# A new step order for the first phase of a fused gated-attention and MLP kernel

## The chip, the cores and the metric

The kernel runs on one core of a Trainium2 chip. The metric is device time in microseconds (us) of one execution, from the first to the last instruction with what lies around them; smaller is better. The kernel before was timed in three runs.

## The reference

Gated linear attention (4 batches, 8 heads, 768 steps, head size 48), followed by an MLP with a squared ReLU, all in float32.

```python
f = 1.0 / (1.0 + np.exp(-f_logit))
for t in range(S):
    state = f[:, :, t, :, None] * state + np.einsum('bhd,bhe->bhde', k[:, :, t], v[:, :, t])
    y[:, :, t] = np.einsum('bhd,bhde->bhe', q[:, :, t], state)
...
x = y.transpose(0, 2, 1, 3).reshape(B * S, H * D)      # 3072 x 384
h = x @ w_in                                           # 384 -> 2048
r = np.maximum(h, 0.0)
return ((r * r) @ w_out).astype(np.float32)            # 2048 -> 384
```

## The kernel before

**Tiling.** The 768 steps are cut into six blocks of 128, each of two chunks of 64. A block's eight heads are four units of two heads; unit n is pair n % 4 of block n // 4. The attention of a unit gives rows of the block's matrix x, which is held as a high and a low half, so that each float32 product is three matmuls. A block's MLP has 16 hidden tiles f of 128 rows: nine matmuls up (three row tiles, three products), squared ReLU, nine matmuls down into three accumulators. Only three pairs of a block have a row tile of their own; the fourth pair's rows are spread over the zero rows of the three tiles by small DMAs.

**Weights.** Both weight matrices come as 64-bit words from the host and are decoded on the chip, 32 tiles of 128x384 (f, input or output side) and a small fourth one for the fourth pair.

**Phases.** The first phase does the attention of blocks 0 and 1 (units 0 to 7) and the hidden tiles 0 to 5 of block 0, with their twelve weight tiles. Its steps are written out by hand, in two strings, FIRST and SECOND. After it, the kernel runs block 1's whole MLP, the rest of block 0's, and blocks 2 to 5, in loops with the later units and the later weights hooked in; that part is the same in both kernels.

**What sets the order.** PE, SP, DVE and ACT execute each queue in the order of the program, so the order of the letters is the order of each queue. A step puts instructions into one queue, some (K, m) into two. Between FIRST and SECOND the PSUM pool of the first units is closed, and the pools for the second up-product bank and the three accumulators are opened. The letters, n being a unit:

| step | engine | what it does |
|---|---|---|
| f, k, L | SP | load of the unit's gates, of keys and queries, of all three (256, 512, 768 KB) |
| v | SP | load of its values (192 KB) |
| G | ACT | sigmoid of the gates (L425) |
| K | DVE, POOL | scan of the gates backwards (L430), two 128x8 clamps on POOL (L435), scaled keys (L436) |
| Q | DVE | reciprocal (L442), scan forwards (L444), scaled queries (L447) |
| m | POOL for units 0, 1, 4, 5; else SP | two copies of rows for the fourth pair (L455) |
| r, s | ACT | copies with the halves crossed: queries (L466), states (L474) |
| T, N | PE, ACT | transposed keys (L480) and their copies (L486, L488) |
| D, S, Y | PE | state sums (L504), scores (L515), outputs (L558, L570), 32, 32 and 48 or 64 small matmuls |
| M, C | DVE | masked scores (L522); states (L537, L542; twice as many instructions in block 1) |
| H, X | ACT, DVE | high and low half of x (L583, L587) |
| g, h | POOL, SP | copies of the fourth pair's rows into the three tiles (L594) |

With n a hidden tile: i, o (SP, L385) load its two weight tiles of 384 KB. The input side is decoded by A (ACT, L144 and L148), I, V (DVE, L154 and L161), c (ACT, L176) and J (DVE, L178); the output side by B, O, Z, d and P in the same way. j0 loads the small fourth tile (224 KB), e, n, t, a, w decode it. u is the up-product (PE, L251) of hidden tiles 0 and 1 from the three own row tiles alone, U completes these two from the fourth tile, or is the whole up-product for later tiles; R (ACT, L261 to L263) is the squared ReLU, E (DVE, L268) its low half, W (PE, L277) the down-product. busy is a run of transposes (L657) without a use.

The queue of a buffer matters too: a unit's values go into one of four buffers, its gates, keys and queries into one of three (unit 4's have one of their own), in the order in which the loads stand in the strings, and a load waits for the last reader of what was there.

Of the kernel before, what the change touches and what calls it, by code (L numbers as in the profile page):

```python
# [67 lines left out]
SIGNED = ()  # L68

FIRST = """  # L70
f0 k0 L1 G0 K0 v0 o4 L2 Q0 busy11 T0 G1 N0 o0 K1 m0 busy3 S0 B4 j0 D0 i1 M0 r0 T1 C0 v1 G2 Q1 v2 s0
o5 busy2 Y0 B0 i5 K2 e0 m1 S1 v3 H0 i0 r1 n0 N1 Q2 o3 T2 B5 D1 L4 O0 r2 S2 M1 N2 C1 A0 D2 m2 t0 X0
D3 a0 v4 C2 s1 i3 I0 s2 Y1 A1 w0 V0 L5 Z0 G4 I1 S3 M2 H1 V1 r3 L6 X1 c1 C3 Y2 A3 K4 s3 v5 c0 v6 H2
M3 T4 o2 G5 X2 N4 J0 i2 Y3 A5 Q4 i4 d0 u0 H3 v7 P0 m4 r4 o1 X3 G6 I3 J1 A2 D4 K5
"""
SECOND = """
U0 A4 S4 I2 R0 T5 C4 u1 M4 s4 E0 N5 V2 Q5 Y4 c2 g3 h3 B1 U1 H4 W0 J2 m5 r5 X4 O1 R1 V3 Z1 D5 I4 S5
d1 E1 B3 U2 P1 C5 c3 B2 M5 W1 J3 s5 V4 K6 R2 Y5 c4 Q6 T6 H5 U3 N6 X5 m6 r6 J4 D6 R3 E2 S6 O2 U4 C6
Z2 s6 M6 d2 E3 Y6 R4 P2 I5 W2 V5 H6 E4 c5 X6 r7 J5 S7 O3 D7 M7 U5 C7 Z3 s7 O4 d3 Y7 Z4 P3 d4 W3 H7
P4 R5 X7 O5 g7 h7 Z5 W4 E5 d5 P5 W5  # L80
"""


# [897 lines left out]
```

## Time and profile before

| | |
|---|---|
| times of three runs | 509.21, 509.71, 511.17 us (median 509.71) |
| span of the profiled execution | 508.9 us; around it, to the median, 0.8 us |
| PE / PEld | busy 489.7 / 390.5 us |
| ACT / DVE / POOL | busy 284.0 / 263.3 / 29.4 us |
| DMA | 41.97 MB |
| first and last product of the first phase's MLP | u0 at 34.50 us; W5 until about 76.4 us |
| granted TensorE clock, mean | 0.998 |

A row of a timeline gives start, length, engine, line, operation, tiles, shapes and count, and in brackets the idle time of the engine before it with what ended it. A row of busy times by stretch gives the stretch, its length, the busy time of PE, PEld (its weight loads), DVE, ACT and POOL with counts, the granted clock, the DMA engines' busy share and GB/s. A busy PE is not a PE at its peak, since matmuls overlap.

### The profile page before, as it was taken

Reading aid. Unit: us, or ns where it says so; the run is one execution under the profiler, and the core shown is the slowest. Engines: PE = TensorE matmul, PEld = TensorE weight load, DVE = VectorE, ACT = ScalarE, POOL = GpSimd, SP = SyncE. Lnnn points to the kernel's source line nnn. Section 1 sums busy time; section 2 is a strip of 40 time slices with the busy share of each in tenths; the row PEclk is TensorE's granted clock in tenths of the full one; section 3 lists DMA queues with packets and bytes.
Section 4 is the critical chain, followed back from the end, with each engine's and each line's share of the span. In section 5 each row is a group of like instructions: output and inputs, shape, how many; then the busy total and the mean of one; then the engine's idle time right before and its main releaser. Section 6 shows DMA issues by size and latency. Waiting matters only on the chain.

```text
span 508.9 us, 11460 instructions
## 1 busy us (share of the span) xinstructions
PE 489.7 (96%) x4831; PEld 390.5 (77%) x4831; DVE 263.3 (52%) x484; ACT 284.0 (56%) x577; POOL 29.4 (6%) x66
## 2 busy tenths in 40 slices
PE   5789899999999999999999999999999999999995
PEld 5667677788777878787778777787777877888884
DVE  7899975999856335645315456225365332211112
ACT  4779746877657443755454754543746444544441
POOL 6112010001000000000000000000000000000000
PEclk9999999999999999999999999999999999999999
DMA  8982025563530206213005313004410001100001
GB/s 297 319 288 70 13 71 179 167 215 100 166 90 14 78 7 180 75 27 89 3 1 138 122 28 90 0 1 115 146 28 11 3 1 33 64 0 1 0 1 67
DMA packets 20508, 41.97 MB, mean 82 GB/s; under 512 B 2672, under 2 KB 6000, under 8 KB 20448
## 3 DMA queue, kind: packets, MB, share of 16 engines
q1 hardware_dynamic: 19856, 40.10, 25.7%
q0 software_dynamic: 448, 0.92, 0.8%
q8 instruction: 40, 0.66, 0.5%
q14 instruction: 20, 0.16, 0.1%
q10 hardware_dynamic: 144, 0.13, 0.1%
HBM read 31.69 MB, written 4.72 MB: 72 GB/s over the span
## 4 chain that ended last, share of the span: by engine, by line
PE 77%; DVE 9%; ACT 5%; DMA 5%; issue 1%; SPq 1%; POOL 0%; DVEq 0%; ACTq 0%; POOLq 0%
PE ph L251 35%; PE po L277 34%; DMA raw<-in_w_dram 5%; PE py L558 2%; PE ds L504 2%; PE ds L515 2%; PE py L570 2%; DVE wa L161 1%; DVE gl L268 1%; PE pk L480 1%; ACT ph L262 1%; DVE w L178 1%; DVE fkq L444 1%; ACT ph L261 1%; ACT gh L263 1%
## 5 line engine op out<-in xcount | busy, mean ns | idle before, releaser
L251 PE MATMUL ph<-x,w 128*128 128x512 f32 x864 | 221.5, 401 | 1.2 <-DVE gl L268 0.7
L251 PEld LDWEIGHTS ph<-x,w 128*128 128x128 f32 x864 | 159.3, 188 | 39.3 <-DVE gl L268 1.1
L277 PE MATMUL po<-gh,w 128*128 128x512 f32 x576 | 180.5, 394 | 0.3 <-DVE w L178 0.3
L268 DVE TENSOR_TENSOR gl<-ph,gh 128x512 fp32r<-128x512 f32 x96 | 66.3, 690 | 187.2 <-ACT gh L263 187.0
L261 ACT ACTIVATE ph<-ph 128x512 f32<-128x512 f32 x96 | 55.8, 582 | 135.2 <-PE ph L251 134.5
L277 PEld LDWEIGHTS po<-gh,w 128*128 128x128 f32 x576 | 108.1, 188 | 26.5 <-DVE w L178 0.6
L277 PE MATMUL po<-gl,w 128*128 128x512 f32 x288 | 114.5, 398 | 0.4 <-DVE gl L268 0.4
L277 PEld LDWEIGHTS po<-gl,w 128*128 128x128 f32 x288 | 54.0, 188 | 14.1 <-DVE gl L268 1.1
L263 ACT CAST gh<-ph 128x512 fp32r<-128x512 f32 x96 | 56.3, 587 | 3.0
L262 ACT ACTIVATE ph<-ph 128x512 f32<-128x512 f32 x96 | 55.9, 582 | 3.0
L435 POOL TENSOR_SCALAR fkq<-fkq 128x8 f32<-128x8 f32 x18 | 11.8, 656 | 324.5 <-DVE fkq L430 324.4
L430 DVE TENSOR_TENSOR_SCAN fkq<-fz,dr 128x520 f32<-128x520 f32 x18 | 22.3, 1238 | 6.4 <-ACT fz L425 6.3
L176 ACT CAST w<-wa 128x384 fp32r<-128x384 f32 (+1 forms) x33 | 16.9, 511 | 13.9 <-DVE wa L165 12.2
L558 PEld LDWEIGHTS py<-sc,vn 64*48 64x48 f32 (+1 forms) x640 | 18.1, 126 | 8.1 <-issue 7.0
L444 DVE TENSOR_TENSOR_SCAN fkq<-fz,dz 128x520 f32<-128x520 f32 x18 | 22.4, 1242 | 0.6
L558 PE MATMUL py<-sc,vn 64*48 64x64 f32 (+1 forms) x640 | 21.5, 222 | 0.7 <-DVE sc L522 0.7
L570 PE MATMUL py<-rx,sx 48*48 48x64 f32 (+1 forms) x320 | 21.0, 217 | 0.2
L522 DVE TENSOR_TENSOR sc<-ds,mask 128x512 f32<-128x512 f32 x24 | 16.5, 687 | 8.3 <-PE ds L515 7.6
L144 ACT ACTIVATE wa<-raw 128x384 f32<-128x384 f32 (+1 forms) x33 | 18.1, 548 | 4.3 <-DMA raw<-in_w_dram 4.3
L570 PEld LDWEIGHTS py<-rx,sx 48*48 48x48 f32 (+1 forms) x320 | 18.2, 127 | 0.6 <-ACT sx L474 0.5
L480 PE MATMUL pk<-ident,fkq 128*128 128x128 f32 x72 | 13.3, 315 | 5.4 <-DVE fkq L436 3.6
L161 DVE SCALAR_TENSOR_TENSOR wa<-raw,wa 128x384 int32<-128x384 int32 (+1 forms) x33 | 18.0, 551 | 0.8
(93 smaller groups left out, 408.0 us busy)
## 6 DMA issues: line engine op xcount, KB each, us to landing
fkq<-in_fkqT_dram SPq DMA_DIRECT2D x17, 768.0 KB, 5.4
raw<-in_w_dram SPq DMA_DIRECT2D x32, 384.0 KB, 4.7
vn<-in_vN_dram SPq DMA_DIRECT2D x24, 192.0 KB, 5.1
out_dram<-ob SPq DMA_DIRECT2D x12, 256.0 KB, 2.1
x<-ys SPq DMA_DIRECT2D x30, 64.0 KB, 2.4
last_kq<-fkq SPq DMA_DIRECT2D x28, 64.5 KB, 2.3
out_dram<-part SPq DMA_DIRECT2D x3, 256.0 KB, 2.1
last_kq<-fkq POOLq DMA_DIRECT2D x8, 64.5 KB, 6.3
```

The costliest lines, as they stand in the source:

```text
L161: nc.vector.scalar_tensor_tensor(out=h, in0=upper, scalar=-(1 << 31), in1=h, op0=ALU.bitwise_and, op1=ALU.bitwise_or)
L251: self.nc.tensor.matmul(self.ph[f], lhsT=w[:, i], rhs=x[:, j], start=first and n == 0, stop=last and n == 2)
L261: nc.scalar.activation(ph, ph, AF.Relu)
L262: nc.scalar.activation(ph, ph, AF.Square)
L263: nc.scalar.copy(out=gh, in_=ph)
L268: self.nc.vector.tensor_tensor(out=gl, in0=self.ph.pop(f), in1=gh.bitcast(F32), op=ALU.subtract)
L277: self.nc.tensor.matmul(self.po[e], lhsT=l, rhs=r, start=f == self.fs[0] and i == 0, stop=f == self.fs[-1] and i == 2,)
L430: V.tensor_tensor_scan(out=rr[:, ::-1], data0=self.fz[:, NZ * CZ : 0 : -1], data1=dr[:, ::-1], initial=0.0, op0=ALU.mult, op1=ALU.add,)
L444: V.tensor_tensor_scan(out=pp, data0=self.fz[:, : NZ * CZ], data1=dz, initial=0.0, op0=ALU.mult, op1=ALU.add)
L480: nc.tensor.transpose(out=self.pk[:, b], in_=self.kt[:, b * TB : (b + 1) * TB], identity=ident)
L558: nc.tensor.matmul(self.py[h * C : h * C + m, c, b * C : (b + 1) * C], lhsT=self.vn[rows, b, h * D : h * D + m], rhs=self.sc[rows, h, b], ...
L570: nc.tensor.matmul(self.py[h * C : h * C + m, c, b * C : (b + 1) * C], lhsT=s[rows, b * D : b * D + m], rhs=q[rows], start=False, stop=b = ...
```

## The change

The two strings are replaced by others. They hold the same 234 steps; 22 steps move from FIRST to SECOND. Nothing else is edited.

```diff
 FIRST = """
-f0 k0 L1 G0 K0 v0 o4 L2 Q0 busy11 T0 G1 N0 o0 K1 m0 busy3 S0 B4 j0 D0 i1 M0 r0 T1 C0 v1 G2 Q1 v2 s0
-o5 busy2 Y0 B0 i5 K2 e0 m1 S1 v3 H0 i0 r1 n0 N1 Q2 o3 T2 B5 D1 L4 O0 r2 S2 M1 N2 C1 A0 D2 m2 t0 X0
-D3 a0 v4 C2 s1 i3 I0 s2 Y1 A1 w0 V0 L5 Z0 G4 I1 S3 M2 H1 V1 r3 L6 X1 c1 C3 Y2 A3 K4 s3 v5 c0 v6 H2
-M3 T4 o2 G5 X2 N4 J0 i2 Y3 A5 Q4 i4 d0 u0 H3 v7 P0 m4 r4 o1 X3 G6 I3 J1 A2 D4 K5
+f0 G0 k0 K0 busy11 L1 G1 Q0 S0 K1 T0 N0 o0 B0 v0 r0 D0 L2 G2 busy3 j0 i0 e0 A0 M0 Q1 C0 S1 s0 i2 T1 o1
+K2 O0 N1 A2 B1 Y0 H0 n0 T2 v1 Q2 i1 I0 v2 I2 Z0 D1 r1 busy2 L4 t0 a0 O1 V0 v3 N2 D2 A1 S2 C1 m2 s1 X0 M1
+Y1 D3 V2 v7 m0 m1 S3 c0 r2 J0 I1 C2 Z1 s2 i3 M2 H1 X1 Y2 c2 V1 G4 K4 A3 I3 M3 d0 H2 X2 o5 r3 L5 i5 d1 C3
 """
 SECOND = """
-U0 A4 S4 I2 R0 T5 C4 u1 M4 s4 E0 N5 V2 Q5 Y4 c2 g3 h3 B1 U1 H4 W0 J2 m5 r5 X4 O1 R1 V3 Z1 D5 I4 S5
-d1 E1 B3 U2 P1 C5 c3 B2 M5 W1 J3 s5 V4 K6 R2 Y5 c4 Q6 T6 H5 U3 N6 X5 m6 r6 J4 D6 R3 E2 S6 O2 U4 C6
-Z2 s6 M6 d2 E3 Y6 R4 P2 I5 W2 V5 H6 E4 c5 X6 r7 J5 S7 O3 D7 M7 U5 C7 Z3 s7 O4 d3 Y7 Z4 P3 d4 W3 H7
-P4 R5 X7 O5 g7 h7 Z5 W4 E5 d5 P5 W5
+s3 J2 c1 G5 u0 T4 N4 o4 Y3 H3 V3 A5 c3 w0 B4 K5 X3 U0 R0 J1 u1 U1 I5 Q4 i4 r4 S4 T5 J3 P0 o2 E0 V5 L6 W0
+Q5 A4 I4 m4 G6 v4 D4 C4 R1 o3 v5 r5 h3 g3 U2 M4 E1 V4 s4 Y4 N5 R2 H4 m5 K6 X4 c4 J4 U3 D5 E2 C5 S5 M5 T6
+B2 O2 U4 R3 N6 s5 B3 P1 Q6 Y5 H5 c5 X5 E3 W1 r6 J5 R4 v6 D6 C6 S6 M6 U5 Z2 m6 s6 Y6 O4 d2 P2 W2 B5 O3 Z3
+H6 X6 Z4 d3 P3 D7 r7 C7 s7 S7 M7 d4 E4 O5 P4 W3 Z5 R5 E5 Y7 H7 X7 g7 h7 d5 W4 P5 W5
 """
```

The queues that the prediction follows, cut out of the strings (before the bar: FIRST):

```
SP   before  f0 k0 L1 v0 o4 L2 o0 j0 i1 v1 v2 o5 i5 v3 i0 o3 L4 m2 v4 i3 L5 L6 v5 v6 o2 i2 i4 v7 o1 | h3 m6 h7
SP   after   f0 k0 L1 o0 v0 L2 j0 i0 i2 o1 v1 i1 v2 L4 v3 m2 v7 i3 o5 L5 i5 | o4 i4 o2 L6 v4 o3 v5 h3 v6 m6 h7
POOL before  K0 K1 m0 K2 m1 K4 m4 K5 | g3 m5 K6 g7
POOL after   K0 K1 K2 m0 m1 K4 | K5 m4 g3 m5 K6 g7
PE   before  busy11 T0 busy3 S0 D0 T1 busy2 Y0 S1 T2 D1 S2 D2 D3 Y1 S3 Y2 T4 Y3 u0 D4 | U0 S4 T5 u1 Y4 U1 W0 D5 S5 U2 W1 Y5 T6 U3 D6 S6 U4 Y6 W2 S7 D7 U5 Y7 W3 W4 W5
PE   after   busy11 S0 T0 D0 busy3 S1 T1 Y0 T2 D1 busy2 D2 S2 Y1 D3 S3 Y2 | u0 T4 Y3 U0 u1 U1 S4 T5 W0 D4 U2 Y4 U3 D5 S5 T6 U4 Y5 W1 D6 S6 U5 Y6 W2 D7 S7 W3 Y7 W4 W5
DVE  after   K0 Q0 K1 M0 Q1 C0 K2 O0 n0 Q2 I0 I2 Z0 t0 O1 V0 C1 X0 M1 V2 J0 I1 C2 Z1 M2 X1 V1 K4 I3 M3 X2 C3 | J2 V3 w0 K5 X3 J1 I5 Q4 J3 P0 E0 V5 Q5 I4 C4 M4 E1 V4 K6 X4 J4 E2 C5 M5 O2 P1 Q6 X5 E3 J5 C6 M6 Z2 O4 P2 O3 Z3 X6 Z4 P3 C7 M7 E4 O5 P4 Z5 E5 X7 P5
ACT  after   G0 G1 N0 B0 r0 G2 e0 A0 s0 N1 A2 B1 H0 r1 a0 N2 A1 s1 c0 r2 s2 H1 c2 G4 A3 d0 H2 r3 d1 | s3 c1 G5 N4 H3 A5 c3 B4 R0 r4 A4 G6 R1 r5 s4 N5 R2 H4 c4 B2 R3 N6 s5 B3 H5 c5 r6 R4 s6 d2 B5 H6 d3 r7 s7 d4 R5 H7 d5
```

## The prediction

> **What bounds the kernel now.** I read the page's engine totals first, then the busy time by stretch.
>
> ```profile
> PE 489.7 (96%) x4831; PEld 390.5 (77%) x4831; DVE 263.3 (52%) x484; ACT 284.0 (56%) x577; POOL 29.4 (6%) x66
> 4.20:31.70 27.50, 19.15 (x419) 16.38 (x420) 23.97 (x40) 17.63 (x44) 7.51 (x15) 1.00 1.01 329
> 31.70:73.60 41.90, 39.64 (x675) 30.68 (x675) 39.85 (x76) 32.78 (x75) 7.32 (x15) 1.00 0.27 72
> 76.40:508.90 432.50, 425.53 (x3718) 339.03 (x3716) 197.28 (x361) 230.85 (x455) 11.16 (x24) 1.00 0.22 66
> ```
>
> The columns are length, then busy time of PE, PEld, DVE, ACT and POOL, granted clock, DMA share and GB/s. From 76.4 us on, PE is 98% busy and the program is the same in both kernels. So the edit can move the end only by moving the moment at which PE starts block 1's products. Until 31.7 us the DMA engines are full (share 1.01). DVE is 87% busy there and 95% from 31.7 to 73.6: the first phase runs on DVE, with PE close behind. DVE's idle time in the two stretches, 3.5 + 2.1 = 5.6 us, is the most that an order can win on DVE. Some of it is the few hundredths between instructions, so I put the ceiling at 4.1 us (below).
>
> Next I read DVE's and ACT's timelines for what DVE waits for.
>
> ```profile
> 9.26 1.24 DVE L430 TENSOR_TENSOR_SCAN fkq<-fz,dr 128x520 f32<-128x520 f32 x1 [0.38 <-ACT fz L425]
> 23.52 0.56 DVE L154 SCALAR_TENSOR_TENSOR wa<-wa,raw 128x384 int32<-128x384 int32 x1 [0.78 <-ACT raw L148]
> 28.01 0.69 DVE L587 TENSOR_TENSOR x<-first_py,x 112x512 fp32r<-112x512 f32 x1 [0.71 <-ACT x L583]
> 13.78 0.56 ACT L144 ACTIVATE wa<-raw 128x384 f32<-128x384 f32 x1 [0.23 <-DMA raw<-in_w_dram]
> 22.32 0.56 ACT L144 ACTIVATE wa<-raw 128x384 f32<-128x384 f32 x1 [1.39 <-DMA raw<-in_w_dram]
> 26.87 0.63 ACT L425 ACTIVATE fz<-fkq 128x512 f32<-128x512 f32 x1 [1.23 <-DMA fkq<-in_fkqT_dram]
> ```
>
> The wait at 23.52 goes back to a load: ACT could start A0 only at 22.32, when weight i0 landed, and DVE's I0 follows it. At 26.87 ACT (gate G4) waited for load L4.
>
> **What one step costs on DVE.** These rows are consecutive steps without a wait: K4, M3, X2, J0, Q4, P0, X3. The fence ends with C4 of block 1, C3 of block 0, and the end of the phase (X7, P5).
>
> ```profile
> 29.40 1.24 DVE L430 TENSOR_TENSOR_SCAN fkq<-fz,dr 128x520 f32<-128x520 f32 x1
> 30.67 0.69 DVE L436 TENSOR_TENSOR fkq<-fkq 128x512 f32<-128x512 f32 x1
> 31.28 0.68 DVE L522 TENSOR_TENSOR sc<-ds,mask 128x512 f32<-128x512 f32 x1
> 31.88 0.68 DVE L587 TENSOR_TENSOR x<-first_py,x 112x512 fp32r<-112x512 f32 x1
> 32.48 0.55 DVE L178 TENSOR_TENSOR w<-wa,w 128x384 fp32r<-128x384 f32 x1
> 32.95 0.20 DVE L442 RECIPROCAL dz<-fkq 128x8 f32<-128x8 f32 x1
> 35.06 0.55 DVE L178 TENSOR_TENSOR w<-wa,w 128x384 fp32r<-128x384 f32 x1
> 35.53 0.68 DVE L587 TENSOR_TENSOR ys<-first_py,ys 112x512 fp32r<-112x512 f32 x1
> ...
> 28.74 0.36 DVE L537 TENSOR_TENSOR sp<-ds,last_kq 112x192 f32<-112x192 f32 x1
> ...
> 49.22 0.35 DVE L537 TENSOR_TENSOR sp<-state,fkq 112x192 f32<-112x192 f32 x1
> 50.73 0.68 DVE L522 TENSOR_TENSOR sc<-ds,mask 128x512 f32<-128x512 f32 x1
> ...
> 70.74 0.69 DVE L587 TENSOR_TENSOR ys<-py,ys 112x512 fp32r<-112x512 f32 x1
> ...
> 73.07 0.56 DVE L178 TENSOR_TENSOR w<-wa,w 128x384 fp32r<-128x384 f32 x1
> ```
>
> From start to start: K 29.40 to 31.28, 1.88; M and X 0.60 each; a decode step 0.47; Q 32.95 to 35.06, 2.11; C 28.74 to 29.40, 0.66 in block 0 and 49.22 to 50.73, 1.51 in block 1. For E (one 128x512 subtraction, like X) I take 0.60, for n0, t0 and w0 (narrower decode steps) 0.33.
>
> **The change, part by part.** It moves steps only, so every term is a wait that goes or comes.
>
> *Loads on SP.* Weights i0, i2, o1, i1 move ahead of v2; o4, o5, i5 move back; L4 comes after 5792 KB instead of 6752 KB. Landings follow the bytes ahead in the queue. At 13.78 the first 3264 KB had landed; i0 now closes 3488 KB, so by 329 GB/s it lands at about 14.5 instead of 22.3. L4, 960 KB earlier, lands about 3.0 us earlier, 23.9. A0 then stands on ACT at 14.6, G4 at 27.3 and I0 on DVE at 19.3, all behind their data. m2 waits on SP for Q2 (19.3), with v7, i3, o5 and L5 queued behind it; before, m2 also held SP until Q2 at 19.0, so I price it at 0. v7 moved ahead of v4 delays v4 by 192 KB, 0.6 us; v4's first reader D4 now comes at 44. Nothing.
>
> *DVE up to X2.* From K1 at 9.26 (still held by load L1) the new queue holds 3 K, 2 Q, 4 M, 3 C, 3 X, 12 decode steps and n0, t0: 5.64 + 4.22 + 2.4 + 1.98 + 1.8 + 5.64 + 0.66 = 22.34, so X2 ends at 31.6. I went through ACT's and PE's queues for each input and found each one early, the nearest being G4 (27.9 for K4 at 28.07) and H1 (26.9 for X1 at 27.0). Before, X2's place ended at 32.48 with six decode steps fewer done and C3 and w0 more: DVE is ahead by 0.9 + 2.82 - 0.99 = 2.7 us.
>
> *u0, T4, Y3, X3.* In the old order PE ran T4 and Y3 before u0; now u0 is first, and K5 stands before X3 on DVE. The PE rows:
>
> ```profile
> 31.42 1.11 PE L480 MATMUL pk<-ident,fkq 128*128 128x128 f32 x4 [0.71 <-DVE fkq L436]
> 34.50 3.11 PE L251 MATMUL ph<-x,w 128*128 128x512 f32 x9
> 37.54 0.68 PE L504 MATMUL ds<-vn,kn 64*64 64x48 f32 x32
> 39.67 0.66 PE L480 MATMUL pk<-ident,fkq 128*128 128x128 f32 x4
> 40.09 2.35 PE L251 MATMUL ph<-x,w 128*128 128x512 f32 x9
> ...
> 52.25 0.34 PE L558 MATMUL py<-sc,vn 64*64 64x64 f32 x8
> ...
> 69.39 0.50 PE L277 MATMUL po<-gl,w 128*128 128x512 f32 x1
> 70.20 0.73 PE L277 MATMUL po<-gh,w 128*128 128x512 f32 x2 [0.31 <-DVE w L178]
> ...
> 76.37 4.36 PE L251 MATMUL ph<-x,w 128*128 128x512 f32 x18
> ```
>
> u0 starts at 31.7 (was 34.50) and takes 3.05; T4 0.42 (39.67 to 40.09); Y3 about 1.2 (block 1's outputs from 52.25 are followed by other work within that); H3 0.6 on ACT. X3 can start at 37.1, but DVE reaches it after C3, J2, V3, w0 and K5 at 35.6. That is a new stall of 1.5 us, and all of DVE's later work is queued behind it. X3 ends at 37.8.
>
> *The rest.* Behind X3 DVE has 22 decode steps, 3 Q, K6, 4 C, 4 M, 6 E and 4 X: 10.34 + 6.33 + 1.88 + 6.04 + 2.4 + 3.6 + 2.4 = 33.0, ending at 70.8. Going through ACT's queue I find half a microsecond of new waits (X4 for H4, which stands behind R2). P5 ends at 71.3 against 73.07 + 0.56 = 73.6. Without any wait it would be 69.5: the ceiling of 4.1. m4 stands ahead of g3 on POOL and waits for Q4 until 41; g3's parts land near 47, where U2 needs the last at 46.7: 0.4 us on PE, taken up by Y4's wait for M4.
>
> *The end of the phase.* Block 1's products need the rows that h7 and g7 copy from X7's output.
>
> ```profile
> 71.46 1.79 SPq L594 DMA_DIRECT2D x<-ys  x3
> 71.72 1.50 POOL L594 DMA_DIRECT2D x<-ys  x3 [17.09 <-DVE ys L587]
> DMA to landing us min/median/max: 2.5/2.8/3.5
> ```
>
> Before, W3, W4 and W5 (from 69.39 to 76.37) covered that trip. Now W3 runs before Y7 and only W4 and W5 cover it. I get W3 66.2 to 68.4, Y7 to 69.6, H7 to 70.2, X7 to 70.95 (was 71.43), W4 and W5 until 74.0. The first tile's copy on POOL, issued 0.3 after X7 and 2.8 under way, is there at 74.05, the last one (0.5 us earlier than before's, needed 1.4 us into the first group) allows a start at 74.25. So block 1 starts at 74.3, not 76.37: **2.1 us earlier**. PE in the stretch behind is full, so I take it to the end one to one. The span of 508.9 becomes 506.8. The runs' median of 509.71 lies 0.8 above that span; I add the same 0.8: 507.6.
>
> [...] Above, the first products of u0 are slow: 3.11 us for nine where the next nine take 2.35, at a granted clock shown as 1.00, and small products before it are slow too:
>
> ```profile
> 21.62 1.03 PE L504 MATMUL ds<-vn,last_kn 64*48 64x48 f32 x26
> ...
> 57.31 0.57 PE L504 MATMUL ds<-vn,kn 64*64 64x48 f32 x29 [0.28 <-DVE x L587]
> ```
>
> [...]
>
> **The rivals.**
> [...]
> *The lead is given back.* The loads of block 1's remaining weights are issued on SP behind h7, so they come only 0.5 us earlier, and block 1's first stages are full on DVE too:
>
> ```profile
> 90.00:100.00 10.00, 9.42 (x41) 7.62 (x42) 9.25 (x22) 8.66 (x21) 0.00 (x0) 1.00 0.56 178
> ```
>
> If DVE's decoding paces that stretch, only 0.5 us is left: 509.2. Against it: PE has 9.42 of 10 there, and ACT's wait for weights is nowhere after 40 us. The same size comes out if the new X7-to-W5 cover is 1.5 us short.
> *Slower: X3 blocks DVE.* Every microsecond that u0 starts late now delays X3 and the 33 us queued behind it, which the old order (X3 at 35.53 with no wait) did not. With P5 2.3 us ahead, u0 at 34.0 leaves nothing, and at 36.6 the kernel is 0.5% slower; u0 at 37.5 gives 513.2. What could hold it: S3 needs rows that m0 and m1 copy, which POOL now issues only after K2 (16 to 18.7). For those POOL copies the page has 6.3 us to landing, so they are there by 25, for S3 at 27.1; they would have to take twice as long.
>
> ```profile
> last_kq<-fkq POOLq DMA_DIRECT2D x8, 64.5 KB, 6.3
> ```
>
> **How the numbers follow.** The forecast (a gain of 1.0 to 3.2, centre 2.1) has 0.41; the warm or stall-free case 0.18; given back or nothing gained 0.27; slower 0.14. A measurement of this kernel tells 0.5%, 2.55 us, from no change. Three in ten of the forecast and nearly all of the second case pass it: faster 0.31 and, since my stalls are rounded up where a row was missing, 0.36; slower 0.14; the same 0.50. The range: the ceiling of 4.1 with 0.3 for a shorter tail gives 505.3; above, the given-back case and half of the slower one, 511.2. The forecast alone runs from 506.5 to 508.7.
>
> **What would show it.** Right: X2 on DVE ends near 31.6 and u0 starts near 31.7; no ACT wait for i0; a DVE gap of about 1.5 us before X3 near 37; P5 ending near 71.3; block 1's first products near 74.3. Wrong: u0 after 34, a gap before X3 over 3 us, a PE gap of over 1 us between W5 and block 1, or a lead at 75 us that is smaller at 110.

## The result, and the profile after

The new order is slower: 516.78 us (median of four runs, 515.26 to 518.06) against 509.92 for the kernel before (four runs). The ratio is 1.0126, 95% interval 1.011 to 1.0142: 6.9 us lost where 2.1 were to be won. The span grew from 508.9 to 514.8 us.

First the busy time by stretch, cut at X2's end, at P5's end and at the start of block 1. (Before, the first cut, at 31.70, lies 0.8 us ahead of X2's end; cut there at X2's end too, DVE's idle time behind it is the same 2.1 us.)

```profile
4.20:33.50 29.30, 18.83 (x420) 15.91 (x421) 26.23 (x44) 17.23 (x44) 7.88 (x15) 0.85 0.95 314
33.50:79.10 45.60, 39.79 (x675) 30.84 (x674) 37.25 (x72) 33.10 (x75) 6.26 (x12) 0.95 0.20 60
81.50:514.80 433.30, 425.95 (x3718) 338.95 (x3717) 197.14 (x361) 230.81 (x455) 11.53 (x24) 1.00 0.22 67
```

The last stretch is 433.3 us long, before 432.5. So 5 of the 6 us are lost ahead of it, as the prediction said they would have to be. DVE's load in the phase is the same (63.5 us, before 63.8), but in the second stretch it now idles 8.4 us (45.60 - 37.25) instead of 2.1. The granted clock is 0.85 and 0.95 in the two stretches of the phase. The 1.00 of the rows before is no proof of full speed there: u0's nine products took 3.11 us, the next nine 2.35.

PE's timeline of the kernel after shows where. The bracket is the idle time in front of the row and what ended it.

```profile
32.13 3.61 PE L250 MATMUL ph<-x,w 128*128 128x512 f32 x9
...
51.94 0.68 PE L503 MATMUL ds<-vn,kn 64*64 64x48 f32 x32
54.52 0.69 PE L514 MATMUL ds<-fkq 48*64 48x64 f32 x32 [1.89 <-DVE state L541]
55.14 0.93 PE L479 MATMUL pk<-ident,fkq 128*128 128x128 f32 x4
55.72 3.74 PE L250 MATMUL ph<-x,w 128*128 128x512 f32 x9
...
64.72 0.69 PE L514 MATMUL ds<-fkq 48*64 48x64 f32 x32 [1.26 <-DVE state L541]
65.35 2.36 PE L250 MATMUL ph<-x,w 128*128 128x512 f32 x9
...
72.97 0.79 PE L514 MATMUL ds<-last_kq 48*64 48x64 f32 x32 [1.26 <-DVE state L541]
...
81.69 4.73 PE L250 MATMUL ph<-x,w 128*128 128x512 f32 x18
```

u0 starts at 32.13 (before 34.50, forecast 31.7), near the forecast, though not for the forecast's reason (below). From 50 us on PE stops three times, ahead of S5, S6 and S7, and each time the row says that DVE's states (L541, step C of the same unit) ended the wait. After the first stop, U4's nine products take 3.74 us instead of 2.35. Block 1 starts at 81.69; before it was 76.37, forecast 74.3.

DVE's side, from its timeline and from the list of waits (total us, times, longest):

```profile
12.91 0.69 DVE L521 TENSOR_TENSOR sc<-ds,mask 128x512 f32<-128x512 f32 x1 [1.98 <-PE ds L503]
...
32.90 0.69 DVE L586 TENSOR_TENSOR x<-first_py,x 112x512 fp32r<-112x512 f32 x1
37.90 0.69 DVE L586 TENSOR_TENSOR ys<-first_py,ys 112x512 fp32r<-112x512 f32 x1 [0.50 <-ACT ys L582]
54.11 0.35 DVE L541 TENSOR_TENSOR state<-sp,ds 112x192 f32<-112x192 f32 x1
55.28 0.69 DVE L521 TENSOR_TENSOR sc<-ds,mask 128x512 f32<-128x512 f32 x1 [0.82 <-PE ds L514]
61.27 0.69 DVE L586 TENSOR_TENSOR x<-py,x 112x512 fp32r<-112x512 f32 x1 [2.25 <-ACT x L582]
78.50 0.55 DVE L177 TENSOR_TENSOR w<-wa,w 128x384 fp32r<-128x384 f32 x1
...
PE ds L514 <- DVE state L541: 4.4, 3, 1.9
DVE sc L521 <- PE ds L503: 2.0, 1, 2.0
```

C5's last instruction ends at 54.46, S5 starts at 54.52. At 12.91 it is the other way round: DVE's M0, which reads only what S0 wrote, waits 1.98 us for D0, whose columns it doesn't read. D, S, M and C of a unit all work in one PSUM tile, `ds`: D writes the columns that C reads, S the columns that M reads. By data, S doesn't depend on C and M doesn't depend on D.

So the theory: **a step waits for every earlier step of the program on another engine that touches the unit's `ds` tile, where one of the two writes it, whatever columns they touch.** Which of the two stands first in the strings then decides who waits, even if both are in different queues. In the old strings D and S stand ahead of M and C in every unit. In the new ones C5, C6, C7 stand ahead of S5, S6, S7, and D0 ahead of M0 with little time between them. The rivals: the new order of the queues is itself slow, and this wait only the place where it shows; X3's blocking of DVE, the prediction's own slower case; or the clock alone.

### The profile page after: what moved, and what is told of

It reads as the page before. It is cut to its first block, busy times and chain, and to the rows that moved or that the text cites. A ratio compares the mean times of both kernels' runs of the same rounds, so it can differ in the third digit from the quotient of the medians.

```text
span 514.8 us, 11462 instructions
## 1 busy us (share of the span) xinstructions
PE 489.6 (95%) x4831; PEld 389.5 (76%) x4831; DVE 262.9 (51%) x484; ACT 283.8 (55%) x577; POOL 30.3 (6%) x66
## 4 chain that ended last, share of the span: by engine, by line
PE 80%; DVE 10%; ACT 4%; DMA 4%; issue 2%; SPq 0%; POOL 0%; ACTq 0%; DVEq 0%; POOLq 0%
PE ph L250 36%; PE po L276 33%; DMA raw<-in_w_dram 3%; PE ds L514 2%; PE ds L503 2%; PE py L557 2%; PE py L569 2%; PE pk L479 1%; DVE gl L267 1%; DVE fkq L443 1%; DVE wa L160 1%; DVE w L177 1%; ACT ph L261 1%; ACT ph L260 1%; ACT gh L262 1%
## 5 line engine op out<-in xcount | busy, mean ns | idle before, releaser
L514 PE MATMUL ds<-fkq 48*64 48x64 f32 x576 | 14.4, 235 | 10.0 <-DVE fkq L446 6.8
L557 PEld LDWEIGHTS py<-sc,vn 64*64 64x64 f32 (+1 forms) x640 | 17.9, 126 | 7.3 <-issue 6.6
L557 PE MATMUL py<-sc,vn 64*64 64x64 f32 (+1 forms) x640 | 21.3, 222 | 0.0
L514 PEld LDWEIGHTS ds<-fkq 48*64 48x64 f32 x576 | 12.0, 144 | 11.4 <-DVE fkq L446 7.6
L582 ACT CAST x<-py 112x512 fp32r<-112x512 f32 x15 | 8.8, 586 | 18.6 <-PE py L569 17.7
```

What stands on the lines that cost most here:

```text
L514: nc.tensor.matmul(self.ds[c * C : (c + 1) * C, h, B * D + b * C : B * D + (b + 1) * C], lhsT=self.kt[rows, cs], rhs=self.ra[rows, cs], st ...
L557: nc.tensor.matmul(self.py[h * C : h * C + m, c, b * C : (b + 1) * C], lhsT=self.vn[rows, b, h * D : h * D + m], rhs=self.sc[rows, h, b], ...
```

## The experiments

Medians of one series share the runs of the kernel before: 510.6 us for the first four kernels, 510.14 us for the last four.

**S ahead of C.** Each queue keeps its instructions and their order; only the two tokens' order in the program changes.

```diff
-... D5 E2 C5 S5 M5 T6 ... D6 C6 S6 M6 ... D7 r7 C7 s7 S7 M7 ...
+... D5 S5 E2 C5 M5 T6 ... D6 S6 C6 M6 ... D7 S7 r7 C7 s7 M7 ...
```

> The changed kernel with S5, S6 and S7 written ahead of C5, C6 and C7 in SECOND. Each queue holds the same instructions in the same order; only which of C and S stands first in the program changes. Theory (a step waits for every earlier step of the program that touches the unit's shared PSUM tile, even other columns of it): PE's idle 1.89, 1.26 and 1.26 us before S5, S6 and S7 go, the half-clock stretch of U4 (1.4 us lost) goes with the first of them, block 1 starts near 75.5 instead of 81.7: about 510.5 us. Rival (the new queue order itself is slow: PE waits for C only because DVE is late, and without this wait the next one takes its place): block 1 starts within 1 us of 81.7, 516 us. Rival (X3 blocks DVE, as the prediction's slower case had it): nothing of its cause is touched, 516.8 us.

Measured: 510.24 us, ratio 0.9995 (0.9983 to 1.0007): 6.5 us come back by the medians (5.3 between the two profiled executions), by a change that no queue sees. PE's timeline at the same place, and at the start of block 1:

```profile
53.69 0.60 PE L503 MATMUL ds<-vn,kn 64*64 64x48 f32 x29
54.19 0.66 PE L514 MATMUL ds<-fkq 48*64 48x64 f32 x30
54.78 0.65 PE L479 MATMUL pk<-ident,fkq 128*128 128x128 f32 x4
55.20 2.35 PE L250 MATMUL ph<-x,w 128*128 128x512 f32 x9
...
76.90 4.68 PE L250 MATMUL ph<-x,w 128*128 128x512 f32 x18 [0.31 <-DMA x<-ys]
```

S5 follows D5 at once, U4 takes 2.35 us, and block 1 starts 4.8 us earlier than in the kernel after. That is 1.4 us later than expected; in this execution u1's nine products took 3.37 us, in the kernel after 2.25. The order of the queues was not what cost, nor X3, which stands where it stood.

**M0 ahead of D0.** Again only the program's order.

```diff
-... r0 D0 L2 G2 busy3 j0 i0 e0 A0 M0 Q1 ...
+... r0 M0 D0 L2 G2 busy3 j0 i0 e0 A0 Q1 ...
```

> The changed kernel with M0 written ahead of D0 in FIRST; the queues are the same instructions in the same order. Theory: DVE's M0 no longer waits for D0 (1.98 us idle at 12.9), so DVE reaches Q1 about 1.7 us earlier and u0 starts about 1 us earlier (31.1 instead of 32.1); the waits for C5 to C7 stay, so at most 1 us at the end: 515.8 us. Rival (the tile is tracked by columns, M0 waits for something else): no change, 516.8 us.

Measured: 515.59 us, ratio 1.0101 (1.0078 to 1.0124). M0 now follows K1 without a wait:

```profile
10.74 0.69 DVE L435 TENSOR_TENSOR fkq<-fkq 128x512 f32<-128x512 f32 x1
11.35 0.68 DVE L521 TENSOR_TENSOR sc<-ds,mask 128x512 f32<-128x512 f32 x1
```

1.2 us less than the kernel after by the medians, 1.3 by the ratios; the intervals of the ratios (1.0078 to 1.0124 and 1.011 to 1.0142) overlap a little, so of its size alone this run is weak.

**Both.**

> Both moves: S5, S6, S7 ahead of C5, C6, C7 and M0 ahead of D0, all queues in the changed kernel's order. Theory: the time forecast for this queue order comes back, 507.6 us to 509.5 us, so not slower than before. Rival (the queue order itself is slow): 515 us or more. Rival (the two waits hide each other): as with the first move alone.

Measured: 508.71 us, ratio 0.9964 (0.9948 to 0.998): faster than before by 1.9 us. From the profile of this kernel:

```profile
9.93 1.24 DVE L429 TENSOR_TENSOR_SCAN fkq<-fz,dr 128x520 f32<-128x520 f32 x1 [1.05 <-ACT fz L424]
32.26 0.34 DVE L536 TENSOR_TENSOR sp<-ds,last_kq 112x192 f32<-112x192 f32 x1
46.04 0.35 DVE L541 TENSOR_TENSOR state<-sp,ds 112x192 f32<-112x192 f32 x1 [1.38 <-PE ds L503]
52.82 0.35 DVE L541 TENSOR_TENSOR state<-sp,ds 112x192 f32<-112x192 f32 x1 [0.15 <-PE ds L514]
71.02 0.68 DVE L586 TENSOR_TENSOR ys<-py,ys 112x512 fp32r<-112x512 f32 x1
71.61 0.55 DVE L177 TENSOR_TENSOR w<-wa,w 128x384 fp32r<-128x384 f32 x1
...
12.60 1.10 PE L503 MATMUL ds<-vn,kn 64*64 64x48 f32 x32 [1.49 <-DVE sc L521]
32.49 0.94 PE L250 MATMUL ph<-x,w 128*128 128x512 f32 x3 [1.20 <-DVE x L586]
74.83 4.61 PE L250 MATMUL ph<-x,w 128*128 128x512 f32 x18 [0.35 <-DMA x<-ys]
```

The waits have not gone, they have changed sides: now it is C5 that waits for S5, for 0.15 us, and D0 that waits for M0, with PE idle for 1.49 us ahead of it. On these sides they cost less: the ratio was 0.9995 with the first move alone, and the two intervals do not overlap. X7 starts at 71.02 and block 1 at 74.83. (The rows at 9.93, 32.26, 32.49 and 46.04 are used further down.)

**The same cause put into the old order.** The kernel before, with C5 and C6 written ahead of S5 and S6 and every queue as it was.

```diff
-... D5 I4 S5 d1 E1 B3 U2 P1 C5 ... D6 R3 E2 S6 O2 U4 C6 ...
+... D5 I4 d1 E1 B3 P1 C5 S5 U2 ... D6 R3 E2 O2 C6 S6 U4 ...
```

> The kernel before, with C5 and C6 written ahead of S5 and S6; its queues hold the same instructions in the same order as before. Theory: the same cause put into the old order makes PE idle before S5 and S6 until C5 and C6 are done. In the old order C5 ends at 60.1 and S5 stood at 57.7, U2 to U5 stand behind: 2.5 us at S5 and about 1.5 us at S6, plus up to 1.4 us if TensorE falls to half clock in the gap: 512 to 515 us. Rival (a wait of S for C is harmless, the new queue order is what costs): 509.9 us, no change.

Measured: 515.21 us, ratio 1.01 (1.0081 to 1.0118), just past the upper end of what was expected. (The expectation's 57.7 and 60.1 are unit 6's rows; in the kernel before S5 starts at 47.2 and C5 ends at 50.8.) PE's timeline:

```profile
50.71 0.69 PE L515 MATMUL ds<-fkq 48*64 48x64 f32 x32 [3.18 <-DVE state L542]
51.34 3.82 PE L251 MATMUL ph<-x,w 128*128 128x512 f32 x9
...
63.01 0.69 PE L515 MATMUL ds<-fkq 48*64 48x64 f32 x32 [1.26 <-DVE state L542]
...
80.88 4.36 PE L251 MATMUL ph<-x,w 128*128 128x512 f32 x18
```

Two pairs of tokens make the old order nearly as slow as the new one: 3.18 and 1.26 us of waiting, U2 in 3.82 instead of 2.37, block 1 4.5 us late.

**The clock.** The kernel after, its waits left in, with seven products of no use (step z6) in the gap between D5 and S5.

```diff
+            for _ in range(7):
+                nc.tensor.matmul(
+                    self.pk.rearrange("p b n -> p (b n)"), lhsT=moe.w[0, 0][:, 0, 0:P],
+                    rhs=self.xs[0][0][:, 0], start=True, stop=True,
+                )
...
-... D5 E2 C5 S5 ...
+... D5 z6 E2 C5 S5 ...
```

> The changed kernel, with the wait of S5 for C5 left in, and seven 128x512 products of no use (into the bank of unit 6's transposes, which overwrite them) between D5 and S5, where PE idles 1.89 us. Theory (the idle stretch makes TensorE fall to half clock, which costs U4 1.4 us): U4's nine products take 2.3 us instead of 3.74 and the end comes 1.0 to 1.4 us earlier, 515.5 us. Rival (the half clock has nothing to do with the gap): U4 stays at 3.7 us and the time is 516.8 us or, with the products in the way, more.

Measured: 514.67 us, ratio 1.009 (1.007 to 1.0111), 1.8 us below the kernel after by the ratios (0.0036 of 510); the two intervals just touch. The profile is plainer than the time:

```profile
53.19 1.88 PE L487 MATMUL pk<-x,w 128*128 128x512 f32 x7
55.14 0.69 PE L523 MATMUL ds<-fkq 48*64 48x64 f32 x32
55.77 0.66 PE L480 MATMUL pk<-ident,fkq 128*128 128x128 f32 x4
56.18 2.34 PE L250 MATMUL ph<-x,w 128*128 128x512 f32 x9
```

S5 still starts late (55.14; D5, too, runs 0.6 us later than in the kernel after), but U4 takes 2.34 us. In the three profiled executions with this gap left empty (the kernel after, M0 ahead of D0, and the old order at its S5) the nine products behind it took 3.74, 3.89 and 3.82 us. The slow U4 was a second price of the wait, not a cause of its own.

**Three versions beyond.** On the kernel with both moves: D4 and its load ahead of W0; six products of no use (step z5) between Y3 and U0; both.

```diff
-... K5 X3 U0 R0 ... E0 V5 L6 W0 Q5 A4 I4 m4 G6 v4 D4 C4 ...
+... K5 X3 z5 U0 R0 ... E0 V5 L6 v4 D4 W0 Q5 A4 I4 m4 G6 C4 ...
```

> The kernel with both moves (S5 to S7 ahead of C5 to C7, M0 ahead of D0), and D4 with its load v4 ahead of W0, so that C4 on DVE no longer waits 1.38 us for D4 behind W0. Theory (DVE sets the pace of the rest of the phase): DVE is 1.3 us earlier from C4 on, PE pays nothing because it is not late there, and 0.5 to 1.2 us arrive at the end: 507.8 us. Rival (PE sets it): no change, 508.7 us.

> The kernel with both moves, and six 128x512 products of no use (into the bank of unit 5's transposes, which overwrite them) between Y3 and U0, where PE idles 1.88 us for X3. Theory (the gap costs the clock): U0 and u1 take 0.9 and 2.3 us instead of 1.65 and 3.10, and up to 1.5 us arrive at the end if PE is the pace there: 507.3 us. Rival (DVE is the pace there, the slow products are hidden): the two are faster, the time stays 508.7 us.

> Both additions at once. Theory (PE and DVE pace the stretch together, each edit alone is held by the other engine): more than the sum of the two alone, up to 2 us, 506.7 us. Rival (one of them is the pace alone): as the better of the two.

Measured: 508.59 us (0.9968, 0.9952 to 0.9984), 507.27 us (0.9946, 0.9927 to 0.9964) and 508.05 us (0.9959, 0.9944 to 0.9975). All are faster than the kernel before; none can be told from the kernel with both moves (0.9948 to 0.998). For D4 the profile has block 1 at 74.03, 0.8 us earlier than 74.83, which the times don't resolve. For the filler I can't claim its 507.27: in the profiled execution U0 and u1 were fast, as expected, but u0 was slow, and block 1 started at 74.95.

```profile
31.68 3.84 PE L250 MATMUL ph<-x,w 128*128 128x512 f32 x9
36.94 1.66 PE L487 MATMUL pk<-x,w 128*128 128x512 f32 x6
38.44 0.93 PE L250 MATMUL ph<-ys,w 112*128 112x512 f32 x3
39.21 2.25 PE L250 MATMUL ph<-x,w 128*128 128x512 f32 x9
```

That both additions together would bring more than their sum was not borne out.

**What stays open.** Whether the waits are kept by the whole tile or by a part of it larger than the columns: `ds` has two halves of 512 columns, and D and S each write columns of both, so no run here tells the two apart. A version with D in the one half and S in the other was not tried.

## Why the prediction was wrong

**The step that failed** is the search for new waits, in two places. The larger stands under *The rest*: "Going through ACT's queue I find half a microsecond of new waits". It put PE's waits for DVE behind X3 at nothing. Measured were 1.89 + 1.26 + 1.26 = 4.4 us of waits of S5, S6 and S7 for C5, C6 and C7, and 1.4 us more for U4 (3.74 us instead of 2.35) at a granted clock of 0.50; the swap of these three pairs alone brought back 6.5 us. The smaller stands under *DVE up to X2*: "I went through ACT's and PE's queues for each input and found each one early". Measured was a wait of 1.98 us of M0 for D0. In both places I took as inputs of a step what it reads by data: S5 the keys and queries, M0 the scores. The list of waits of the kernel before shows such a wait:

```profile
DVE sc L522 <- PE ds L504: 0.7, 2, 0.5
```

M (L522) reads only the columns of the scores, and yet D (L504) ended its wait, twice (M1, 0.21 us, and M7, 0.49). At 0.7 us in all I passed over it. Read as a rule it would have sent me to the strings for every D, S, M and C of one unit, and C5 ahead of S5 is plain there. "It moves steps only, so every term is a wait that goes or comes" was right; but I took the order of two tokens in different queues to be without effect, and it decides who waits.

No run here shows what would happen without such a wait.

**Point by point.**
- *Loads.* The wait for i0 went, as forecast, and DVE idled 29.30 - 26.23 = 3.1 us up to X2, of it 1.98 for M0. (In another profiled execution with D0 ahead of M0, that of S ahead of C, it was 1.3.)
- *X2 and u0.* X2 ended at 33.5 instead of 31.6, most of it M0's wait, forecast as none. That u0 still started at 32.13 (forecast 31.7) was luck: the forecast set u0 right behind X2, but its first six products need only the first two row tiles. Without M0's wait alone it started at 31.14:

```profile
31.14 3.85 PE L250 MATMUL ph<-x,w 128*128 128x512 f32 x9
```

  In the kernel with both moves it started at 29.62, and only its last three products waited for X2 (the row at 32.49).
- *X3.* Forecast a stall of 1.5 us; measured 0.50, since DVE came late itself. X3 started at 37.90 (forecast 37.1). The prediction's own steps from X2 to X3 add up to 3.8 us, so DVE would have been there at 35.4 and not 35.6; with that, P5 without any wait comes to about 69.1, and the ceiling of 4.1 should have been 4.5.
- *The rest.* Forecast half a microsecond of new waits; measured, in the kernel after, M5 0.82 and X5 2.25 among them, all behind S5's wait. In the kernel with both moves this step comes out right but for a microsecond: P5 ended at 72.2 (forecast 71.3), block 1 started at 74.83 (74.3), with a 0.35 us wait for the copies of X7's rows.
- *The size.* 2.1 us forecast for this order of queues; 1.9 us measured once S and M0 no longer waited. In that kernel DVE took 32.26 - 9.93 = 22.33 us from K1 to X2's end, where 22.34 were forecast: the costs of the steps were right, the list of who waits for whom was not. That the sizes agree so well is in part luck, since two errors offset each other there: the stall of 1.5 us before X3 did not come (X3 started at 36.06 without a wait), and C4 waited 1.38 us for D4, where the forecast had nothing.

**The rivals.** The slower case, with a chance of 0.14, had the right sign and the wrong mechanism: u0 was not late, and X3 blocked DVE by half a microsecond. Nor was a lead given back in block 1's stages: the kernel after had none, and with both moves block 1 started 1.5 us earlier than before and the time was 1.9 us shorter.

**The warm case.** In "the warm or stall-free case", to which the prediction gives 0.18, warm meant a u0 of 2.1 us instead of 3.05, with 506.7 us for the whole: my estimate; no run shows u0 at 2.1. The runs showed this in its place. In the kernel after, PE was busy for all of the 3.42 us up to 21.25, and D2's first 29 products then took 0.60 us, where 26 at 21.62 in the kernel before had taken 1.03. But the granted clock fell from 1.0 to 0.50 at 24.66 (worked out below), and u0 took 3.61 us.

```profile
23.88 0.60 PE L503 MATMUL ds<-vn,kn 64*64 64x48 f32 x29 [1.85 <-ACT kn L485]
```

In the profiled execution with both moves u0's products were fast (the first six took 1.67 us, the last three 0.94, at a granted clock of 1.00), and the time of that execution was 509.46, not 506.7.

## What to carry to other kernels

Where a framework derives the waits, the order of the program is more than the order of each queue: of two steps in different queues that touch one PSUM tile, the one written later waited for the other here (S5 for C5, 1.89 us; M0 for D0, 1.98 us), though they share no byte. Before costing a reordering, list for every shared tile which steps swap places in the program, and price each swap as a wait of the one for the other. Swapping back hands the wait to the other engine: here C5 for 0.15 us instead of S5 for 1.89. So write the step of the engine that must not stop first. And look at the small odd waits in the list (a step that waits for a result it doesn't read): they show the rule before an edit makes it expensive.

## What the hardware showed that I had not expected

A gap of 1.89 us on PE cost more than itself here: U4's nine products behind it took 3.74 us, and 2.34 with the gap filled. These are stretches of the kernel after, three of them 3.41 us long, about as long as the half clock around U4 lasted (worked out below): the 3.41 us ahead of two falls of the clock, the 3.41 us ahead of S6, where it didn't fall, and the fall and the return around U4 (length, then busy PE, PEld, DVE, ACT, POOL, then granted clock).

```profile
51.97:55.38 3.41, 1.52 (x67) 1.33 (x67) 2.42 (x7) 2.19 (x4) 0.48 (x1) 1.00 0.00 0
21.25:24.66 3.41, 1.56 (x82) 1.27 (x78) 3.38 (x9) 2.17 (x8) 0.00 (x0) 1.00 0.59 138
61.31:64.72 3.41, 2.15 (x39) 1.48 (x37) 3.05 (x7) 3.26 (x8) 0.00 (x0) 1.00 0.01 2
...
55.00:56.00 1.00, 1.00 (x21) 0.93 (x12) 0.72 (x2) 0.00 (x0) 0.00 (x0) 0.69 0.06 16
56.00:58.70 2.70, 2.70 (x8) 2.13 (x7) 2.63 (x5) 2.52 (x7) 0.00 (x0) 0.50 0.00 0
58.00:59.00 1.00, 1.00 (x4) 0.82 (x3) 0.97 (x2) 0.81 (x3) 0.00 (x0) 0.60 0.00 0
```

A mean of 0.69 from 55 to 56 puts the fall from 1.0 to 0.5 at 55.38 (0.38 + 0.62 x 0.5), a mean of 0.60 the return at 58.80: 3.42 us at half clock. The fall came after 3.41 us with PE busy for 1.52 (1.56 the other time); with 2.15 of 3.41 busy it did not come. The other fall came at 24.66 (the mean from 24 to 25 is 0.83), 30.72 us before this one, which is nine times 3.41. That time the clock stayed at half for three such stretches, until 34.90 (the mean from 34 to 35 is 0.55), with PE busy for 2.92, 2.73 and 3.41 us of them and a granted clock of 0.50 in each. In the profiled execution with both moves it fell at 36.68, ahead of U0 (the mean from 36 to 37 is 0.84), after 1.65 us of 3.41 busy. The falls are not the same in every execution: the mean granted clock of the four timed runs of the kernel after was 0.982 to 0.995. Whether a share of busy time decides the fall, no run here shows.

In the fall at 55.38 a gap of 1.89 us, with work on both sides of it in the 3.41 us before the fall, was enough.
